# A gated attention and token-MLP block: output projection transposed, 512 tokens a matmul

## The chip, the core and the metric

The kernel runs on one core of a Trainium2 chip. The core has a matrix engine (TensorE, PE in the rows; its weight loads are PEld), VectorE (DVE), ScalarE (ACT), GpSimd (POOL), and a queue engine SyncE (SP) that only issues DMAs; 16 DMA engines move the data. The metric is the time of one execution on the device in microseconds (us).

## The reference

`x` is 2048 tokens by 640 channels. The output mixes attention and a token-mixing MLP by a gate of each token:

```python
g = _sigmoid((x * gate_w).sum(-1, keepdims=True))
a = _A_ref(x, A_wqkv, A_wo)            # 32 heads of 20 channels; softmax(q k^T * 20**-0.5) v, then @ wo
b = _B_ref(x, B_w1, B_b1, B_w2, B_b2)  # layernorm; gelu(h^T w1 + b1) w2 + b2 over the tokens
return g * a + (1 - g) * b
```

All of it is float32. The kernel keeps the precision by splitting a value into a high and a low part: a product of two split matrices takes three matmul passes (high by high, high by low, low by high).

## The kernel before

Names: P is 128, S the 2048 tokens, D the 640 channels, NC = 5 chunks of 128 channels, NT = 16 tiles of 128 tokens, HALF = 320 channels, LAST = the 4 last heads. The order of every engine's instructions is written out by hand, so each engine takes its instructions in the order of the program.

Stages, with their time in the profiled execution:

1. Up to about 222 us: the projections to q, k and v, the gate `g_t` (one value a token, tokens on the partitions), `omg` = 1 - g, and `b2o` = b2 (1 - g). Matmuls of q and k are 128x128 weights by 512 tokens (L55).
2. 222 to about 727 us: the MLP, in two halves `d` of 320 channels. In each half a phase u (w1) is followed by a phase y (w2) with 16 tiles of 128 tokens. Between its matmuls TensorE works ahead on the score maxima: matmuls `s` (L212) into four PSUM banks, which VectorE (L218, L237) or ScalarE (L227) reads. ScalarE evacuates a y tile (L708, L632), scaled by `omg` and with `b2o` added, GpSimd adds the two partial sums into `ty` (L705), and 4 us later in the planner's clock (`later_on(4000, ...)`) SyncE stores the tile to `y_d` in DRAM (L706). SyncE's queue also carries the weight loads `wr` (L518).
3. 727 to about 1699 us: the attention loop, 16 pairs of heads by 32 iterations. An iteration has four score matmuls `st`, their exponentials on ScalarE (L1022, L1030), two `s` matmuls with their maxima on VectorE until iteration 8 of the last pair, and the `pv` matmuls (L919). The row sums of the softmax go to `l_d`, the products to `o_d`; `norm_steps` makes reciprocals of the sums and stores them, broadcast to 20 rows a head, in `r_d`. In the last pair the loop also loads (`e_load`, `y_load`) and splits (`e_high`, `e_low`) what the projection needs first, and `first_row` works off the first token tile's passes with matmuls of two 64-row halves (`pair64`, L49).
4. From 1699 us: the output projection, the tail. `a_tile(t, cs)` takes 128 tokens of the normalised attention output as weights and 320 columns of `wo` as moving data, two PSUM banks a tile, four banks in turn. The attention output comes as `or` times `rb` (reciprocals), multiplied by VectorE (L966), copied to the high part by ScalarE (L968), and subtracted to the low part by VectorE (L974). The fifth chunk (k = 4) holds the last heads, whose sums are known only after the loop: `last_load`, `last_recip`, a store to `rc_d` (L881), four broadcast loads (`l_rest`, L999). Token tiles 1 to 7 therefore run four chunks first and the fifth later. VectorE evacuates with `g` times PSUM plus `oy`, the stored MLP tile (L1130), and SyncE stores 128 tokens by 640 channels of the output.

Of the kernel before, what the change touches and what calls it, by code (L numbers as in the profile page):

```python
# [13 lines left out]
P = 128  # L14
# [17 lines left out]
def gated_mix(ctx, tc, xT, x, wqk, wv0, wv1, wo, w1, w1t, b1, w2, b2, out):  # L32
# [34 lines left out]
    y_d = dram.tile([S, D], F32, name="y_d")  # L67

# [401 lines left out]
    nc.vector.tensor_mul(b2o, b2_t, omg)  # L470
    nc.scalar.activation(ssq, ssq, AF.Gelu_apprx_tanh)
# [381 lines left out]

    def norm_steps(h0, h1):
        b = (h1 - h0) * S // P
        a = S // b
        rl = ap.tile([P, 256], F32, tag="rl", bufs=1, name=f"rl{h0}")

        def load():
            nc.gpsimd.dma_start(rl[:, :b], l_d[h0:h1].rearrange("h (a b) -> (h a) b", b=b))  # L860

        def recip(i):
            nc.vector.reciprocal(rl[:, i: i + 64], rl[:, i: i + 64])
# [7 lines left out]
    last_rl = []  # L871

    def last_load():
        b = LAST * S // P
        rl = ap.tile([P, 256], F32, tag="rl", bufs=1, name="rl_last")
        nc.sync.dma_start(rl[:, :b], l_d[H - LAST:].rearrange("h (a b) -> (h a) b", b=b))
        last_rl.append(rl[:, :b])
# [12 lines left out]
    def pv_evac(p, qh, pv):  # L890
# [13 lines left out]
        if qh == 1 and p in (7, 11, 13, 15):  # L904
            h0 = {7: 0, 11: 16, 13: 24, 15: 28}[p]
# [27 lines left out]
    o_raw, o_hl, l_hl = {}, {}, {}  # L933

    def o_tiles(q, k, n, tag, bufs, names, pool, dt):
        if pool is lp:
            return [lp.tile([P, k, n], dt, tag="sq", bufs=4, name=f"{name}{tag}{q}") for name in names]
        return [pool.tile([P, k, n], dt, tag=name + tag, bufs=bufs, name=f"{name}{tag}{q}") for name in names]

    def o_load(q, rows, k, n, tag, bufs):  # L940
        raw, rb = o_tiles(q, k, n, tag, bufs, ("or", "rb"), ap, F32)
        cols = slice(q * n, (q + 1) * n)
        o_raw[q, tag] = raw, rb
        for dst, src in ((raw, o_d[rows]), (rb, r_v[rows])):
            nc.sync.dma_start(dst, src.rearrange("(c p) s -> p c s", p=P)[:, :, cols])

    tys = {}

    def y_load(t):
        if 6 <= t < 10:  # L950
            ty = q4([P, D], F32, f"oy{t}")
        else:
            n = t if t < 6 else t - 4
            if n % 3 == 0:
                shape, name = [P, 3, D], f"oy{t}"
                big_y[0] = k8(shape, F32, name) if t < 6 else lp.tile(shape, F32, tag="sk", bufs=2, name=name)
            ty = big_y[0][:, n % 3]
        tys[t] = ty
        nc.sync.dma_start(ty, y_d[t * P:(t + 1) * P, :])

    big_y = [None]

    def o_high(q, k, n, tag, bufs, pool, hi_eng):
        raw, rb = o_raw[q, tag]
        oh, ol = o_tiles(q, k, n, tag, bufs, ("oh", "ol"), pool, F32R)
        nc.vector.tensor_mul(raw, raw, rb)  # L966
        if hi_eng is nc.scalar:
            nc.scalar.activation(oh, raw, AF.Copy)  # L968
        else:
            hi_eng.tensor_copy(oh, raw)  # L970
        return oh, ol

    def o_low(q, tag, hl, eng):
        eng.tensor_sub(hl[1], o_raw.pop((q, tag))[0], hl[0].bitcast(F32))  # L974

    def e_load(q):
        o_load(q, slice(0, (NC - 1) * P), NC - 1, 256, "e", 2)

    def e_high(q, pool, eng=nc.scalar):
        o_hl[q] = o_high(q, NC - 1, 256, "e", 2, pool, eng)  # L980

    def e_low(q, eng=nc.vector):
        o_low(q, "e", o_hl[q], eng)
# [3 lines left out]
    def l_load():  # L987
# [5 lines left out]
        for q in range(4):  # L993
            o_raw[q, "l"] = raw[:, q:q + 1], rb[:, q * 512:(q + 1) * 512].unsqueeze(1)
# [38 lines left out]
    row_mms, row_ps, row_evacs = [], [], []  # L1033

    def row_half(c):
        row_ps[:] = [s_tile([P, HALF], f"a0_{c}_{k}") for k in range(2)]
        oh, ol = o_hl[0]
        cols = slice(c * HALF, (c + 1) * HALF)
        passes = [e for k in range(NC - 1) for e in ((oh[:, k, :P], woh[k]), (oh[:, k, :P], wol[k]), (ol[:, k, :P], woh[k]))]
        for i, (a, b) in enumerate(passes):  # L1040
            row_mms.append((list(row_ps), a, b[:, cols], i == 0, i == len(passes) - 1))
# [173 lines left out]
```

## Time and profile before

| | us |
|---|---|
| three runs: lowest, median, highest | 1778.77, 1779.09, 1782.85 |
| profiled execution | 1777.0 |
| its span, first to last instruction | 1775.2 |
| TensorE busy in the span | 1765.1 (99%) |
| ScalarE busy | 1483.9 (84%) |
| VectorE busy | 1225.5 (69%) |
| GpSimd busy | 658.3 (37%) |

The span is what the trace shows; 1.8 us of the profiled execution lie around it. A matmul's busy time is modelled and longer than its share of the engine: matmuls overlap, so the distance between the starts of two of them is what one costs. A row of a timeline gives the start in us from the span's begin, the time from there to the end of the last instruction that it merges, and how many (x2).

### The profile page before, as it was taken

What the parts mean: (1) busy time and instruction counts of PE and PEld (TensorE: products, weight loads), DVE (VectorE), ACT (ScalarE), POOL (GpSimd) and SP (SyncE); (2) the same over time, 40 slices, a digit from 0 to 9 for tenths busy, and PEclk for the clock granted to TensorE, in tenths of its full rate; (3) what the DMA queues carried; (4) which work ended last, traced back from release to release, by engine and by line L of the source; (5) the groups of instructions that cost most, each with busy time, mean ns of one, the idle gap of its engine ahead of it and who ended that gap; (6) DMA issues with size and microseconds to landing.
All of it is one profiled execution on the core that took longest, in us unless ns stands there. A gap on an engine that the chain in (4) does not pass through costs nothing.

```text
span 1775.2 us, 39545 instructions
## 1 busy us (share of the span) xinstructions
PE 1765.1 (99%) x15000; PEld 1091.8 (62%) x15000; DVE 1225.5 (69%) x2380; ACT 1483.9 (84%) x2566; POOL 658.3 (37%) x989
## 2 busy tenths in 40 slices
PE   9999999999999999999999999999999999999999
PEld 6998899999999999533333333333333333333378
DVE  5303289988899889777777676776767777767245
ACT  4344388888888886799999999999999999999930
POOL 1223577789877777211211111121322121212300
PEclk9999999999999999999999999999999999999999
DMA  8767876567675564334213234043353242301553
GB/s 294 251 196 244 275 179 173 144 176 206 177 195 146 159 179 145 94 67 111 65 41 85 50 72 92 12 112 68 52 136 72 50 94 59 76 15 45 198 132 135
DMA packets 155513, 225.20 MB, mean 127 GB/s; under 512 B 66420, under 2 KB 93444, under 8 KB 151640
## 3 DMA queue, kind: packets, MB, share of 16 engines
q1 hardware_dynamic: 136698, 191.70, 39.4%
q0 software_dynamic: 15888, 25.76, 6.1%
q10 hardware_dynamic: 2736, 5.21, 1.1%
q8 instruction: 118, 1.93, 0.5%
q14 instruction: 73, 0.60, 0.1%
HBM read 166.88 MB, written 55.36 MB: 125 GB/s over the span
## 4 chain that ended last, share of the span: by engine, by line
PE 95%; DMA 3%; DVE 1%; issue 0%; POOL 0%; ACT 0%; SPq 0%; DVEq 0%; ACTq 0%; POOLq 0%
PE pv L919 29%; PE st L1015 22%; PE s L212 12%; PE y L49 10%; PE u L49 9%; PE qk L55 6%; PE v L55 4%; PE a L1124 2%; DMA wr<-in_wqk_dram 1%; DMA xr<-in_xT_dram 1%; DMA rbe<-r_d 0%; DMA rc_d<-rl_last 0%; DMA k_d<-evh 0%; DVE oy L1130 0%; PE a L49 0%
## 5 line engine op out<-in xcount | busy, mean ns | idle before, releaser
L218 DVE TENSOR_REDUCE mx<-s 128x1 f32<-128x512 f32 x1280 | 834.8, 686 | 285.7 <-PE s L212 153.1
L1030 ACT ACTIVATE p<-st 128x512 f32<-128x512 f32 x1022 | 563.9, 619 | 0.0
L919 PE MATMUL pv<-p,v 128*32 128x512 f32 x4088 | 546.2, 605 | 0.0
L1022 ACT ACTIVATE p<-st 128x1024 f32<-128x1024 f32 x511 | 533.1, 1043 | 1.6 <-PE s L212 1.1
L1015 PEld LDWEIGHTS st<-qs_True,ks_True 62*128 62x128 f32 x2044 | 245.3, 185 | 433.9 <-ACT p L1022 425.9
L1015 PE MATMUL st<-qs_True,ks_True 62*128 62x512 f32 x2044 | 494.8, 446 | 0.1
L212 PE MATMUL s<-ks_False,qs_False 60*128 60x512 f32 x1152 | 362.3, 391 | 0.3 <-ACT ov L227 0.2
L44 POOL TENSOR_TENSOR wl<-wr,wh 128x512 fp32r<-128x512 f32 x228 | 275.6, 1220 | 63.9 <-ACT wh L41 52.0
L237 DVE CUSTOM_DVE_ANT_0 ov<-s,ov 128x512 f32<-128x512 f32 x384 | 263.9, 687 | 34.2 <-PE s L212 22.6
L212 PE MATMUL s<-sk,sq 60*128 60x512 f32 x896 | 281.6, 394 | 0.0
L227 ACT ACTIVATE ov<-s 128x512 f32<-128x512 f32 x384 | 228.6, 597 | 62.4 <-PE s L212 53.4
L49 PE MATMUL y<-gh,wh 64*128 64x320 f32 x896 | 225.0, 307 | 0.0
L49 PE MATMUL y<-gl,wh 64*128 64x320 f32 x832 | 216.8, 306 | 0.0
L49 PE MATMUL y<-gh,wl 64*128 64x320 f32 x832 | 216.5, 305 | 0.0
L900 POOL DMA_DIRECT2D l_d<-oev x124 | 60.8, 497 | 409.5 <-DVE oev L892 406.8
L212 PEld LDWEIGHTS s<-ks_False,qs_False 60*128 60x128 f32 x1152 | 210.4, 184 | 3.0 <-ACT ov L227 0.8
L49 PE MATMUL u<-hh,wh 64*128 64x320 f32 x864 | 206.9, 304 | 0.0
L49 PE MATMUL u<-hl,wh 64*128 64x320 f32 x864 | 206.7, 304 | 0.0
L919 PEld LDWEIGHTS pv<-p,v 128*32 128x32 f32 x4088 | 81.6, 108 | 187.3 <-issue 174.2
L49 PE MATMUL u<-hh,wl 64*128 64x320 f32 x800 | 194.4, 304 | 0.0
L41 ACT ACTIVATE wh<-wr 128x512 fp32r<-128x512 f32 (+3 forms) x247 | 146.9, 599 | 42.8 <-PE y L49 15.2
L212 PEld LDWEIGHTS s<-sk,sq 60*128 60x128 f32 x896 | 166.2, 186 | 15.3 <-DVE mx L218 0.4
(149 smaller groups left out, 2449.1 us busy)
## 6 DMA issues: line engine op xcount, KB each, us to landing
wr<-in_w_dram SPq DMA_DIRECT2D x192, 256.0 KB
ks_True<-k_d SPq DMA_DIRECT2D x96, 160.0 KB
qs_True<-q_d SPq DMA_DIRECT2D x192, 80.0 KB
qs_False<-q_d SPq DMA_DIRECT2D x96, 80.0 KB
v_d<-vt SPq DMA_DIRECT2D x32, 212.0 KB
sk<-k_d SPq DMA_DIRECT2D x42, 160.0 KB
sq<-q_d SPq DMA_DIRECT2D x84, 80.0 KB
v<-v_d SPq DMA_DIRECT2D x15, 424.0 KB
```

The source lines that it names most:

```text
L41: nc.scalar.activation(hi, src, AF.Copy)
L44: (lo_eng or nc.vector).tensor_sub(lo, src, hi.bitcast(F32))
L49: nc.tensor.matmul(ps[k], a[r], b[r], start=start, stop=stop)
L55: nc.tensor.matmul(ps, a, b, start=(i == 0 and k == 0), stop=(i == n - 1 and k == 2))
L212: nc.tensor.matmul(ps, qs[half][r, t * P:(t + 1) * P], ks[r, kc * 512:(kc + 1) * 512], start=True, stop=True)
L218: nc.vector.tensor_reduce(mx[:, slot, j, t: t + 1], ps, axis=AX.X, op=OP.max)
L227: nc.scalar.activation(over[j, kc], ps, AF.Relu)
L237: nc.vector.tensor_tensor_reduce(ov, ps, ov, 1.0, -3.0e38, OP.add, OP.max, mx[:, slot, j, t: t + 1])
L919: nc.tensor.matmul(pv[r: r + 32, :], v_tiles[p][:, kt, VW * j: VW * j + 32], pt[j, c], start=(kt == 0), stop=(kt == NT - 1))
L1015: nc.tensor.matmul(ps, ks[r, kt * P:(kt + 1) * P], qs[qh][r, c * 512:(c + 1) * 512], start=True, stop=True)
L1022: nc.scalar.activation(pt, ps, AF.Exp, scale=SCALE)
L1030: nc.scalar.activation(pt, ps, AF.Exp, scale=SCALE)
```

## The change

The projection is computed transposed: 128 channels of `wo` are the weights, 512 tokens of the attention output the moving data, and the kernel's output is [640, 2048], which the host turns back as a view. So the MLP's part must come transposed too. `y_flip` turns each `ty` in blocks of 32x32 on VectorE before the store to `y_d`; `y_turn` then turns the order of the blocks with DMAs from DRAM to DRAM on GpSimd's queue (two in each of the pairs 1 to 10). A gate value now belongs to a column, so it can't be a scalar of the evacuation: it is stored to `g_d`, loaded in the layout of the softmax sums (`load_g`) and multiplied into the reciprocals; the evacuation becomes an add. `norm` runs at pair 3 as well, with eight heads each time, since the reciprocals' tile is half as wide. The first units in the loop are two units of 512 tokens (channel tiles 0 and 1, four chunks) in place of the two halves of the first token tile. In the tail `a_bank` rotates over eight PSUM banks, `last_recip` and `l_rest` come earlier and `rc_d` is stored by SyncE's queue. The last unit runs as two of 256 tokens.

```diff
+    def y_flip(t, d, ty):
+        tt = hp.tile([P, HALF], F32, tag="tt", bufs=2, name=f"tt{d}_{t}")
+        nc.vector.transpose(tt, ty)
+        nc.sync.dma_start(y_d[t * P:(t + 1) * P, d * HALF:(d + 1) * HALF], tt)
...
-            later_on(4000, lambda: nc.sync.dma_start(y_d[t * P:(t + 1) * P, d * HALF:(d + 1) * HALF], ty))
+            later_on(4000, lambda: y_flip(t, d, ty))
...
         def recip(i):
-            nc.vector.reciprocal(rl[:, i: i + 64], rl[:, i: i + 64])
+            c = slice(i, i + 64)
+            nc.vector.reciprocal(rl[:, c], rl[:, c])
+            nc.vector.tensor_mul(rl[:, c], rl[:, c], gls[b][:, c])
...
     def last_recip():
-        nc.vector.reciprocal(last_rl[0], last_rl[0])
-        nc.gpsimd.dma_start(rc_d.rearrange("h (a b) -> (h a) b", b=LAST * S // P), last_rl[0])
+        rl = last_rl[0]
+        nc.vector.reciprocal(rl, rl)
+        nc.vector.tensor_mul(rl, rl, gls[LB][:, :LB])
+        nc.sync.dma_start(rc_d.rearrange("h (a b) -> (h a) b", b=LB), rl)
...
+    def y_turn(j):
+        nc.gpsimd.dma_start(yT_d[32 * j: 32 * j + 32].rearrange("p (u c) -> p u c", c=32),
+                            y_d[:, 32 * j: 32 * j + 32].rearrange("(u p) c -> p u c", p=32))
...
+    def l_split(*qs):
+        for q in qs:
+            o_mul(q, 2)
+            o_high(q, 2)
+        for q in qs:
+            o_low(q, 2)
+
+    def a_passes(ct, q, ks):
+        out = []
+        for k in ks:
+            oh, ol = [t[:, k % 2] for t in o_hl[q, k // 2]]
+            wh, wl = [w[k][:, ct * P:(ct + 1) * P] for w in (woh, wol)]
+            out += [(wh, oh), (wl, oh), (wh, ol)]
+        return out
...
             if p == NP - 1:
-                if it in (0, 16, 26, 30):
-                    e_load((0, 16, 26, 30).index(it))
-                if 13 <= it < 13 + NT:
-                    y_load(it - 13)
-                if it in (5, 24):
-                    e_high(it // 24, ap, nc.gpsimd)
-                    e_low(it // 24, nc.gpsimd)
+                if it in (0, 1, 13, 16, 25, 29):
+                    n = (0, 1, 13, 16, 25, 29).index(it)
+                    e_load(n // 2, n % 2)
+                if it in (2, 3, 14, 17, 19, 21):
+                    y_load((2, 3, 14, 17, 19, 21).index(it))
+                if it in (5, 7, 20, 23):
+                    e = ((0, 0), (0, 1), (1, 0), (1, 1))[(5, 7, 20, 23).index(it)]
+                    o_mul(*e)
+                    o_high(*e, nc.gpsimd)
+                    o_low(*e, nc.gpsimd)
+            elif 1 <= p < 11 and it in (8, 24):
+                y_turn(2 * (p - 1) + it // 24)
...
+    def a_unit(ct, q, ks, parts=1):
+        passes = a_passes(ct, q, ks)
+        y = yts[ct, q]
+        for i in range(parts):
+            ps = a_bank(f"a{ct}_{q}_{ks[0]}_{i}")
+            c = slice(512 * i // parts, 512 * (i + 1) // parts)
+            for n, (a, b) in enumerate(passes):
+                nc.tensor.matmul(ps[:, c], a, b[:, c], start=(n == 0), stop=(n == len(passes) - 1))
+            nc.vector.tensor_add(y[:, c], y[:, c], ps[:, c])
+            if ks[-1] == NC - 1:
+                put = (nc.scalar if i else nc.sync).dma_start
+                put(out[ct * P:(ct + 1) * P, q * 512 + c.start: q * 512 + c.stop], y[:, c])
+
+    most, full, rest = range(NC - 1), range(NC), range(NC - 1, NC)
     last_rb = l_load()
...
+    o_mul(2, 0)
+    o_mul(2, 1)
+    a_unit(2, 0, most)
+    last_recip()
+    l_rest(last_rb)
+    a_unit(3, 0, most)
+    a_unit(4, 0, most)
+    for kp in range(2):
+        o_high(2, kp)
+    for kp in range(2):
+        o_low(2, kp)
+        e_load(3, kp)
+    for ct in range(4):
+        a_unit(ct, 1, most)
+    l_split(0, 1)
+    a_unit(4, 1, most)
+    for kp in range(2):
+        o_mul(3, kp)
+        o_high(3, kp)
+    for q in (2, 3):
+        for ct in range(NC):
+            a_unit(ct, q - 2, rest)
+            if q == 2 and ct == 0:
+                l_split(2)
+            if q == 2 and ct == 2:
+                for kp in range(2):
+                    o_low(3, kp)
+            if q == 2 and ct == 4:
+                l_split(3)
+            a_unit(ct, q, full, 2 if (ct, q) == (NC - 1, 3) else 1)
```

In the new code `q` counts groups of 512 tokens, `ct` channel tiles of 128, and `kp` pairs of chunks (kp = 2 is the fifth chunk alone).

## Rows read from the trace of the kernel before

**Rows 1.** Stretches: length, busy (instructions) of five engines, clock, DMA share, GB/s.
```profile
400.00:500.00 100.00, 100.00 (x1240) 99.73 (x1240) 89.49 (x227) 84.02 (x169) 87.72 (x100) 1.00 0.71 192
...
800.00:1000.00 200.00, 200.00 (x1478) 67.92 (x1480) 140.75 (x229) 200.00 (x317) 29.07 (x64) 1.00 0.33 76
...
1699.00:1776.00 77.00, 70.36 (x456) 66.97 (x456) 43.28 (x70) 8.83 (x10) 3.69 (x7) 0.98 0.50 154
```
**Rows 2.** Timeline of PE in the tail: start, us, instruction, count, idle before.
```profile
1698.92 0.56 PE L1124 MATMUL a<-woh,ohe 128*128 128x320 f32 x2
1699.33 0.46 PE L1124 MATMUL a<-wol,ohe 128*128 128x320 f32 x2
...
1716.33 0.46 PE L1124 MATMUL a<-woh,ole 128*128 128x320 f32 x2
1717.69 0.78 PE L1124 MATMUL a<-woh,ohe 128*128 128x320 f32 x2 [0.90 <-DVE oy L1130]
...
1771.13 0.31 PE L1124 MATMUL a<-woh,oll 128*128 128x320 f32 x1
```
**Rows 3.** Timeline of PE in the q and k projections.
```profile
149.72 0.39 PE L55 MATMUL qk<-xh,wl 128*128 128x512 f32 x1
...
157.96 0.39 PE L55 MATMUL qk<-xh,wl 128*128 128x512 f32 x1
```
**Rows 4.** Timeline of DVE in the tail.
```profile
1724.01 1.22 DVE L966 TENSOR_TENSOR ore<-ore,rbe 128x1024 f32<-128x1024 f32 x1 [3.57 <-DMA rbe<-r_d]
1725.15 1.00 DVE L1130 SCALAR_TENSOR_TENSOR oy<-a,g_t,oy 128x320 f32<-128x320 f32 x2
1726.07 1.28 DVE L966 TENSOR_TENSOR orl<-orl,rbl 128x512 f32<-128x512 f32 x2
```
**Rows 5.** Groups by line and shape, whole span: busy us, mean ns, idle before.
```profile
L44 POOL TENSOR_TENSOR wl<-wr,wh 128x512 fp32r<-128x512 f32 x196 | 252.4, 1298 | 55.3 <-ACT wh L41 46.0 <-PE s L212 6.7 <-POOL xm L487 1.0
...
L180 DVE STREAM_TRANSPOSE mt<-mc 128x32 f32<-128x32 f32 x32 | 6.5, 202 | 1.2 <-POOL mc L44 1.2
...
L968 ACT ACTIVATE ohl<-orl 128x512 fp32r<-128x512 f32 x4 | 2.5, 634 | 7.3 <-DVE orl L966 7.3
```
**Rows 6.** Timelines of POOL and SP (its queue) in the tail.
```profile
1705.92 0.58 POOL L881 DMA_DIRECT2D rc_d<-rl_last x1 [0.98 <-DVE rl_last L880]
...
1713.34 1.42 SPq L999 DMA_DIRECT2D rbl<-rc_d  x4
```
**Rows 7.** Timeline of all engines at the tail's end.
```profile
1771.47 1.01 DVE L1130 SCALAR_TENSOR_TENSOR oy<-a,g_t,oy 128x320 f32<-128x320 f32 x2 [3.83 <-PE a L1124]
...
1772.52 0.35 ACTq L1133 DMA_DIRECT2D out_dram<-oy  x1
```
**Rows 8.** Timeline of ACT in the last pair: first exponential of some iterations.
```profile
1648.27 1.03 ACT L1022 ACTIVATE p<-st 128x1024 f32<-128x1024 f32 x1
...
1650.37 1.03 ACT L1022 ACTIVATE p<-st 128x1024 f32<-128x1024 f32 x1
...
1652.26 1.03 ACT L1022 ACTIVATE p<-st 128x1024 f32<-128x1024 f32 x1
...
1682.40 1.24 ACT L1022 ACTIVATE p<-st 128x1024 f32<-128x1024 f32 x1
...
1684.30 1.24 ACT L1022 ACTIVATE p<-st 128x1024 f32<-128x1024 f32 x1
```
**Rows 9.** Timelines of PE and DVE in the first y phase.
```profile
414.36 0.39 PE L212 MATMUL s<-ks_False,qs_False 60*128 60x512 f32 x1
...
416.13 0.39 PE L212 MATMUL s<-ks_False,qs_False 60*128 60x512 f32 x1
...
415.21 0.69 DVE L218 TENSOR_REDUCE mx<-s 128x1 f32<-128x512 f32 x1
```
**Rows 10.** SP's waits: who, for whom, us in all, times, longest.
```profile
SPq L706 <- POOL ty L705: 103.6, 30, 6.5
```
**Rows 11.** DMA queue of GpSimd, whole span: packets, MB, share of 16 engines.
```profile
q0 software_dynamic: 15888, 25.76, 6.1%
```

More of the change, by code (lines that the diff above doesn't have):

```diff
@@ L852, in gated_mix, with load_g @@
     s_src[NDIFF + 1] = s_stack(NDIFF + 1)
+    gls = {}
+    def load_g(b):
+        gls[b] = ap.tile([P, P], F32, tag="gl", bufs=1, name=f"gl{b}")
+        a = S // b
+        for i in range(P // a):
+            nc.gpsimd.dma_start(gls[b][a * i: a * (i + 1), :b], g_d.rearrange("t p -> (t p)").rearrange("(a b) -> a b", b=b))
     def norm_steps(h0, h1):
@@ L932, in gated_mix @@
     r_v = r_d.rearrange("h d s -> (h d) s")
[L933 to L945, printed above, removed]
@@ L973, in o_low, with e_load @@
[L973 to L983, printed above, removed]
+    o_raw, o_hl = {}, {}
+    def e_load(q, kp):
+        raw, rb = [ap.tile([P, 2, 512], F32, tag=n, bufs=2, name=f"{n}{q}_{kp}") for n in ("ore", "rbe")]
+        o_raw[q, kp] = raw, rb
+        for dst, src in ((raw, o_d), (rb, r_v)):
+            nc.sync.dma_start(dst, src[kp * 256: kp * 256 + 256].rearrange("(c p) s -> p c s", p=P)[:, :, q * 512:(q + 1) * 512])
@@ new lines, in o_mul, with o_high @@
+    def o_mul(q, kp):
+        raw, rb = o_raw[q, kp]
+        nc.vector.tensor_mul(raw, raw, rb)
+    def o_high(q, kp, eng=nc.scalar):
+        raw, _ = o_raw[q, kp]
+        if kp == 2:
+            oh, ol = [ap.tile([P, 1, 512], F32R, tag=n, bufs=4, name=f"{n}{q}") for n in ("ohl", "oll")]
+        elif q % 2:
+            oh, ol = [lp.tile([P, 2, 512], F32R, tag="sq", bufs=4, name=f"{n}{q}_{kp}") for n in ("oh", "ol")]
+        else:
+            oh, ol = [ap.tile([P, 2, 512], F32R, tag=n + "e", bufs=2, name=f"{n}{q}_{kp}") for n in ("oh", "ol")]
+        o_hl[q, kp] = oh, ol
+        if eng is nc.scalar:
+            eng.activation(oh, raw, AF.Copy)
+        else:
+            eng.tensor_copy(oh, raw)
@@ new lines, in o_low, with y_load @@
+    def o_low(q, kp, eng=nc.vector):
+        oh, ol = o_hl[q, kp]
+        eng.tensor_sub(ol, o_raw.pop((q, kp))[0], oh.bitcast(F32))
+    yts = {}
+    def y_turn(j):
+        nc.gpsimd.dma_start(yT_d[32 * j: 32 * j + 32].rearrange("p (u c) -> p u c", c=32),
+                            y_d[:, 32 * j: 32 * j + 32].rearrange("(u p) c -> p u c", p=32))
+    def y_load(n):
+        ct, i = (n, 0) if n < 4 else (4, n - 4)
+        w = S if ct < 4 else S // 2
+        if ct < 2:
+            t = k8([P, w], F32, f"yt{n}")
+        elif ct < 4:
+            t = lp.tile([P, w], F32, tag="sk", bufs=2, name=f"yt{n}")
+        else:
+            t = q4([P, w], F32, f"yt{n}")
+        nc.sync.dma_start(t, yT_d[ct * P:(ct + 1) * P, i * w:(i + 1) * w])
+        for q in range(w // 512):
+            yts[ct, i * 2 + q] = t[:, q * 512:(q + 1) * 512]
@@ L1031, in st_one, with row_unit, evac @@
         pts[g][j, 1] = pt
[L1033 to L1039, printed above, removed]
+    row_mms, row_evacs = [], []
+    def row_unit(ct):
+        ps = [s_tile([P, 512], f"a{ct}_0_{k}") for k in range(2)]
+        passes = a_passes(ct, 0, range(NC - 1))
         for i, (a, b) in enumerate(passes):
-            row_mms.append((list(row_ps), a, b[:, cols], i == 0, i == len(passes) - 1))
-        def evac(ps=list(row_ps)):
+            row_mms.append((ps, a, b, i == 0, i == len(passes) - 1))
+        def evac():
             for k in range(2):
-                nc.vector.scalar_tensor_tensor(tys[0][:, cols], ps[k], g_t[:, :1], tys[0][:, cols], op0=OP.mult, op1=OP.add)
+                nc.vector.tensor_add(yts[ct, 0], yts[ct, 0], ps[k])
         row_evacs.append(evac)
@@ L1139, in gated_mix @@
[L1139 to L1165 removed]
+    banks, two = [0], [None]
@@ new lines, in a_bank @@
+    def a_bank(name):
+        n = banks[0] % 8
+        banks[0] += 1
+        if n == 3:
+            two[0] = psum.tile([P, 2, 512], F32, tag="two", bufs=1, name=name)
+        if n in (3, 4):
+            return two[0][:, n - 3]
+        if n in (5, 6):
+            return s_tile([P, 512], name)
+        return psum.tile([P, 512], F32, tag={0: "one0", 1: "one1", 2: "s3", 7: "pv"}[n], bufs=1, name=name)
+    def a_unit(ct, q, ks, parts=1):
[10 more added lines that the diff above has]
+                put(out[ct * P:(ct + 1) * P, q * 512 + c.start: q * 512 + c.stop], y[:, c])
```

105 lines of the change are left out of this document (18 added, 87 removed).

## Prediction

> **What bounds the kernel now.** I read the windows by stage first. In the MLP TensorE is busy all of 100 us while VectorE has 10.5 us free and GpSimd 12; in the attention loop ScalarE is busy 200 of 200; in the tail, from 1699 us, only TensorE matters, ScalarE and GpSimd being almost idle [rows 1]. So the three stages have three limits: TensorE, ScalarE, TensorE. The change takes work from the tail and adds some to the other two.
>
> Next the timeline of TensorE in the tail. Its matmuls of 320 columns stand 0.1466 us apart: 58 steps of two between 1699.33 and 1716.33 [rows 2]. There are 456: tiles 1 to 7 take 12 passes each, tiles 8 to 15 take 15, the eight late chunks 3 each, 228 passes by two halves. That is 66.8 us. From the first start at 1698.92 to the end of the last slot at 1771.28 are 72.4 us [rows 2], so 5.5 us are gaps; the widest kind has PE waiting for VectorE's evacuation, since only four banks turn [rows 2].
>
> **The tail, part by part.** *Matmuls.* Eight units of 12 passes, ten of 3 and ten of 15 are 276 matmuls of 512 columns, the last 15 of them run as 30 of 256. The trace has the same form in the q and k projections, 128x128 weights by 512 columns: 36 steps from 149.72 to 157.96, 0.2289 us each [rows 3]. 261 of them are 59.7 us. For 256 columns I have only bounds: 0.119 us on the line through both widths, 0.1466 if a step never falls below that of 320. I take the line, the 30 then cost 3.6 us (up to 4.4). Together 63.3 us, 3.5 less than 66.8. Most of it is work moved into the loop: 24 passes of 512 columns there in place of 24 of 640.
>
> *Gaps.* Eight banks give VectorE seven units of time, so the waits for an evacuation should go. One new wait takes their place. The unit of channel tile 0 and tokens 1024 to 1535 is the first that needs the fifth chunk of its quarter, split by `l_split(2)`. The units before it, 84 + 12 + 3 passes, and its own first 12 are 111 steps: TensorE wants that split at 1698.92 + 25.41 = 1724.3. VectorE, in its written order after the evacuation's input of the seventh unit at 1718.2, has: that add, four operations of `l_split(0, 1)`, the next add, two `o_mul` of 1024 elements, one more add, then the multiply wanted. Operations of 512 elements come 0.6 us apart (two in 1.28), one of 1024 takes 1.14 to the next start [rows 4]; I price an add of 512 from PSUM like them. Eight of 0.6 and two of 1.14 end at 1725.3, with 0.2 us in which an add waits for its unit at 1725.5. ScalarE's copy takes 0.63 [rows 5], so TensorE starts the chunk near 1726.3, and the low part, 0.65 later, costs the third pass another 0.2. The stall is 2.2 us. Its bounds: nothing, and the present 5.5. Gaps then save 3.3 us.
>
> This holds only if the fifth chunk's loads are there. Before, the store `rc_d` went out at 1705.92 on GpSimd's queue and its readers at 1713.34 [rows 6], 7.4 us among two transfers that were issued ahead. Now it goes out on SyncE's, a microsecond sooner, ahead of the last two `e_load`s, and they can't go before VectorE's `o_low(2, ...)` near 1710. Their 2 MB at the 154 GB/s of the tail's average [rows 1] would need 14 us, to 1724, just past the 1722 and 1723 at which `o_mul(3, ...)` wants them; the tail's average includes idle time, so I count nothing, and keep 2 us for the range.
>
> *End.* Now two evacuations, 1.01 us, follow the last matmul, then the last issue at 1772.52 and the landing until 1775.2 [rows 7]. After the change one add of 256 elements follows it. From 0.6 for 512 I estimate 0.4, so 0.6 us less.
>
> **The loop.** ScalarE's first exponentials stand 1.89 us apart with a pair of `s` matmuls of 512 columns in the iteration, and 1.90 with a pair of 320 of the first units [rows 8]. The wider pairs are 24 times 0.082 = 2.0 us of TensorE; since an equal pair of `s` fits under ScalarE, nearly all hides. Three iterations carry two pairs; I take 0.5, between 0 and 2.0. An `o_mul` among the maxima cost one iteration 2.10 instead of 1.89 [rows 8]; the change has a second one there: 0.2. The two later ones come after the last maximum, and the loads for all four are issued before they are due, behind no waiting instruction of SyncE but the `m_d` ones that wait already. The multiplies by the gate are seven of 64 columns under idle VectorE: nothing.
>
> **The MLP.** 32 transposes of 128x320. The nearest row is the same operation on 32 columns, 0.202 us [rows 5]; with a column a cycle more, as in the step of 0.6 us per 512 above, 320 columns take about 0.5 us, 0.8 if twice that. One comes in every tile of 8 us, in which VectorE has 0.84 us free [rows 1]. It also has room in the banks: even a late read, 415.21 to 415.90 of the matmul at 414.36, is 0.23 us ahead of that bank's next matmul at 416.13 [rows 9], most by more. So a transpose of 0.5 can push TensorE by at most 0.3, and the free time takes most of that: I take 0.5 us in all, between 0 and 16 (nothing hidden). At the end of the MLP the last tile's transpose is ahead of the loop's first maxima on VectorE: 0.3 us (0 to 0.5). Who waits behind: `y_d`'s store on SyncE, which already waits 3.5 us a tile for GpSimd's add [rows 10], will wait some 2 to 4 us more for VectorE, and the weight loads queued behind it start later. ScalarE does not wait for those loads now; I count nothing, with up to 3 us kept.
>
> *GpSimd's DMAs.* A `y_turn` is 2048 pieces of 128 bytes. GpSimd's queue took 6.1% of 16 times 1775 us for 15888 packets [rows 11], 0.109 us a packet; at that price one turn is 14 us of the 16 engines and two fill 28 of a pair's 61 us, where a third is used [rows 1]. Nobody waits for them before the last pair. The store of the gate is as many pieces, once, in the projections. I take nothing, up to 2 us.
>
> **Sum.** -3.5 - 3.3 - 0.6 + 0.5 + 0.2 + 0.5 + 0.3 = -5.9 us: the span goes from 1775.2 to 1769.3, the profiled execution from 1777.0 to 1771.1. The median of the runs shown lies 2.1 above that execution; carried to it, 1779.1 becomes 1773.2.
>
> **Rivals.** *A wait takes the stall's place* (0.14): the last `e_load`s or `rc_d` land 2 to 4 us late, VectorE stands at `o_mul(3, ...)`, and `l_split(2)` behind it: about -3, 1776. For it speaks that such loads made VectorE wait 3.57 us before [rows 4]; against it that they now share the engines with less.
>
> *The transposes fall on TensorE* (0.06), slower. Place: both y phases. If VectorE had to wait for GpSimd's running operation, 1.30 us long [rows 5] and there 0.88 of the time [rows 1], each transpose would hold VectorE 0.5 + 0.57. What the bank's room of 0.23 and half of the 0.84 free don't take, 0.42 us, TensorE pays: 32 times that is 13 us, in place of 0.5: 1786. It decides from the point where a transpose holds VectorE for more than the 0.65 that these two take. Against it: the 32-column transposes average 0.202, half of them in the MLP beside a busy GpSimd [rows 1, 5]. The Trainium skill has this as a rule ("SBUF — State Buffer", section "SBUF: two separate sides"): VectorE in a two-port mode and GpSimd share a port pair by an exclusive lock, and the later one blocks. By that rule the time would be the 1786; the trace does not show it for the short transposes.
>
> *Late weight loads* (0.07): if the store's wait makes some splits late, +2 to +6 us against the sum, 1777 (0.05 within, 0.02 slower). *GpSimd is held* (0.03): a turn at iteration 8 stands ahead of the maxima's negation, which VectorE's transposition four iterations later waits for; if a turn keeps GpSimd more than some 18 us, every pair loses the rest, tens of us: above 1790. *More gain* (0.08): no stall at `l_split(2)`, nothing in the loop: -8 to -9, 1770.5.
>
> **Chances and range.** The forecast has 0.62, its own range -8 to -3.5, 1771 to 1775.5. A measurement can tell about 0.3%, 5.3 us, from no change. Of the forecast's chance 0.38 lie beyond that, since its centre does, and 0.24 within. Faster: 0.38 + 0.08 = 0.46. Same: 0.24 + 0.14 + 0.05 = 0.43. Slower: 0.06 + 0.02 + 0.03 = 0.11. The range from 1769 to 1780 leaves out the two slow rivals and the ends of the others.
>
> **What would show it.** In the changed profile: matmuls of the projection 0.229 us apart, TensorE's tail from start to last matmul near 65.5 us instead of 72.4, with one gap of about 2 us some 25 us into it that VectorE ends by `l_split(2)`; 32 transposes of about 0.5 us with VectorE near 95% busy in the y phases; an unchanged iteration of 1.90 us. It is wrong if gaps of more than 4 us remain in the tail, if the transposes take over 0.8 us, or if the loop begins later than 0.5 us after its present start.

## The result, and the profile after

The change made the kernel slower: 1785.83 us median (1784.11 to 1793.39, 8 runs) beside 1778.37 us for the kernel before on the same chip, a ratio of 1.0041 with a 95% interval of 1.0027 to 1.0054. In a second group it was 1.0044 (1.0029 to 1.0058). The prediction, 1773.2 us in a range of 1769 to 1780, has the wrong sign. The profiled execution took 1786.21 us, its span is 1783.8 us, 8.6 longer than before.

Where they came from is read from the starts of the same work in both traces. The operations of TensorE are the same up to the loop, so the lag of the n-th matmul can be followed:

| start of | before, us | after, us | lag | new in this stage |
|---|---|---|---|---|
| first u matmul (end of the projections) | 218.03 | 221.53 | 3.50 | **+3.50** |
| 131st u matmul | 230.87 | 237.53 | 6.66 | **+3.16** |
| first y matmul | 346.29 | 352.95 | 6.66 | 0.00 |
| 1401st y matmul (second y phase) | 612.40 | 620.34 | 7.94 | **+1.28** |
| 2561st y matmul (last tile) | 724.02 | 732.40 | 8.38 | +0.44 |
| first exponential of the loop's iterations | 727.31 | 735.68 | 8.37 | 0.00 |
| last pv matmul | 1698.40 | 1708.17 | 9.76 | +1.39 |
| last matmul of the tail | 1771.13 | 1779.88 | 8.75 | **-1.01** |
| end of the span | 1775.2 | 1783.8 | 8.55 | -0.2 |

The tail gained 1.0 us where 6.8 were forecast, and 6.66 us were lost in the first 232 us, where the forecast had counted nothing.

Stretches of the trace after (columns as in [rows 1]):

```profile
226.00:228.00 2.00, 0.11 (x3) 0.09 (x2) 0.88 (x2) 0.81 (x3) 1.26 (x1) 1.00 0.57 118
228.00:230.00 2.00, 2.00 (x18) 2.00 (x20) 1.48 (x5) 1.94 (x4) 1.05 (x1) 0.68 1.02 364
230.00:232.00 2.00, 2.00 (x17) 2.00 (x16) 1.16 (x3) 0.65 (x2) 1.48 (x2) 0.50 0.98 350
...
400.00:500.00 100.00, 100.00 (x1239) 99.72 (x1237) 92.66 (x241) 84.60 (x170) 88.27 (x100) 1.00 0.67 188
800.00:1000.00 200.00, 200.00 (x1480) 67.92 (x1472) 141.04 (x229) 200.00 (x318) 42.18 (x83) 1.00 0.40 92
1708.50:1784.00 75.50, 66.00 (x292) 52.19 (x291) 36.06 (x50) 6.74 (x8) 3.09 (x6) 1.00 0.41 129
```

VectorE's share in the y phase rose from 89.5 to 92.7% [rows 1], with TensorE at 100 as before: the transpositions are hidden there. In the tail TensorE is busy 66.0 of 75.5 us. And at 226 us TensorE stands for almost 2 us, then runs at a granted clock of 0.68 and 0.50 in the next two stretches (0.50 is the lower level, 1.2 GHz).

Timelines of POOL and SP (its queue), after:

```profile
141.56 1.19 POOL L473 DMA_DIRECT2D g_d<-g_t  x1 [6.58 <-DVE omg L471]
157.15 0.61 POOL L490 TENSOR_SCALAR xm<-xm,negm,rstd 128x320 f32<-128x320 f32 x1 [14.40 <-DMA xm<-in_x_dram]
...
145.72 0.44 SPq L330 DMA_DIRECT2D q_d<-evl  x1
146.21 0.46 SPq L485 DMA_DIRECT2D xm<-in_x_dram  x1
147.11 2.11 SPq L330 DMA_DIRECT2D q_d<-evh  x1
157.58 0.32 SPq L330 DMA_DIRECT2D q_d<-evl  x1
...
1657.03 2.38 POOL L983 TENSOR_TENSOR ol<-ore,oh 128x1024 fp32r<-128x1024 f32 x1
...
1722.34 1.67 SPq L1018 DMA_DIRECT2D rbl<-rc_d  x4
...
1725.51 0.78 SPq L961 DMA_DIRECT2D rbe<-r_d  x1
```

Timeline of DVE, after:

```profile
144.19 0.69 DVE L44 TENSOR_TENSOR evl<-qk,evh 128x512 fp32r<-128x512 f32 x1
156.86 0.69 DVE L44 TENSOR_TENSOR evl<-qk,evh 128x512 fp32r<-128x512 f32 x1 [11.99 <-DMA q_d<-evl]
...
1654.63 1.22 DVE L965 TENSOR_TENSOR ore<-ore,rbe 128x1024 f32<-128x1024 f32 x1
...
1658.42 2.07 DVE L965 TENSOR_TENSOR ore<-ore,rbe 128x1024 f32<-128x1024 f32 x1
...
1735.53 1.23 DVE L965 TENSOR_TENSOR ore<-ore,rbe 128x1024 f32<-128x1024 f32 x1 [0.49 <-DMA rbe<-r_d]
1736.67 0.68 DVE L1164 TENSOR_TENSOR yt<-yt,a 128x512 f32<-128x512 f32 x1
1737.27 0.69 DVE L965 TENSOR_TENSOR orl<-orl,rbl 128x512 f32<-128x512 f32 x1
```

The gate's store goes out at 141.56. The stores of q that SyncE issues behind it, and the loads of `xm`, do not land until about 157: VectorE stands 12 us for a buffer that a `q_d` store still reads, GpSimd gets its first `xm` at 157.15. In the kernel before the same evacuation and the same first `xm` stand at (timelines of DVE and POOL, before)

```profile
146.66 0.69 DVE L44 TENSOR_TENSOR evl<-qk,evh 128x512 fp32r<-128x512 f32 x1 [2.25 <-ACT evh L41]
146.97 0.62 POOL L487 TENSOR_SCALAR xm<-xm,negm,rstd 128x320 f32<-128x320 f32 x1 [13.23 <-DMA xm<-in_x_dram]
```

From 145 to 149 us the core's DMAs moved 3 and 19 GB/s (two stretches of 2 us), 247 and 311 in the kernel before. What the DMA list says of the store (KB, us from issue to landing):

```profile
g_d<-g_t POOLq DMA_DIRECT2D x1, 8.0 KB, 14.3
```

Timeline of PE, after, with what answers [rows 2]:

```profile
227.92 0.50 PE L214 MATMUL s<-ks_False,qs_False 60*128 60x512 f32 x1 [1.89 <-ACT ov L229]
...
1708.69 0.50 PE L1163 MATMUL a<-oh,woh 128*128 128x512 f32 x1
1709.03 0.39 PE L1163 MATMUL a<-oh,wol 128*128 128x512 f32 x1
1709.26 0.40 PE L1163 MATMUL a<-ol,woh 128*128 128x512 f32 x1
...
1735.61 0.39 PE L1163 MATMUL a<-ol,woh 128*128 128x512 f32 x1
1738.67 0.50 PE L1163 MATMUL a<-ohl,woh 128*128 128x512 f32 x1 [2.67 <-ACT ohl L977]
...
1743.64 0.40 PE L1163 MATMUL a<-oll,woh 128*128 128x512 f32 x1
1744.82 0.51 PE L1163 MATMUL a<-ohl,woh 128*128 128x512 f32 x1 [0.78 <-DVE yt L1164]
...
1779.88 0.28 PE L1163 MATMUL a<-oll,woh 128*128 128x256 f32 x1
```

Two kinds of gap are to be seen: the stall at the split of tokens 1024 to 1535 (1735.61 to 1738.67), and a wait for VectorE's add, here 1743.64 to 1744.82, which comes four times: starts 1.30, 1.18, 1.17 and, with 256 columns, 0.79 us apart.

Groups, SyncE's waits and GpSimd's queue, after, which answer [rows 5], [rows 10] and [rows 11]:

```profile
L700 DVE STREAM_TRANSPOSE tt<-ty 128x320 f32<-128x320 f32 x32 | 16.1, 504 | 0.0
```
```profile
SPq L701 <- DVE tt L700: 139.4, 31, 8.2
```
```profile
q0 software_dynamic: 17392, 31.06, 7.2%
```

The queue has 1504 packets more than in [rows 11], though twenty turns and the store, each of 2048 pieces, were added: a packet of this list is not a piece.

### The profile page after: what moved, and what is told of

The parts are those of the page before. It is cut to its first block, busy times and chain, and to the rows that moved or that the text cites. A ratio compares the mean times of both kernels' runs of the same rounds, so it can differ in the third digit from the quotient of the medians.

```text
span 1783.8 us, 39291 instructions
## 1 busy us (share of the span) xinstructions
PE 1766.7 (99%) x14835; PEld 1079.3 (61%) x14835; DVE 1231.4 (69%) x2401; ACT 1480.5 (83%) x2564; POOL 692.5 (39%) x1026
## 4 chain that ended last, share of the span: by engine, by line
PE 84%; DMA 3%; DVE 2%; POOL 0%; issue 0%; ACT 0%; SPq 0%; ACTq 0%; DVEq 0%
PE pv L941 28%; PE st L1043 22%; PE s L214 12%; PE u L49 10%; PE y L49 9%; PE a L1163 2%; DVE mx L220 1%; DMA q_d<-evl 1%; DMA k_d<-evl 1%; DMA rbe<-r_d 1%; DMA rc_d<-rl_last 0%; DMA xm<-in_x_dram 0%; PE a L49 0%; DMA k_d<-evh 0%; DVE evl L44 0%
## 5 line engine op out<-in xcount | busy, mean ns | idle before, releaser
L214 PE MATMUL s<-ks_False,qs_False 60*128 60x512 f32 x1152 | 357.1, 393 | 2.7 <-ACT ov L229 2.5
L214 PEld LDWEIGHTS s<-ks_False,qs_False 60*128 60x128 f32 x1152 | 206.6, 185 | 6.3 <-ACT ov L229 3.4
L49 PE MATMUL u<-hl,wh 64*128 64x320 f32 x864 | 199.3, 305 | 0.0
L49 PE MATMUL u<-hh,wh 64*128 64x320 f32 x864 | 199.3, 305 | 0.0
L49 PE MATMUL u<-hh,wl 64*128 64x320 f32 x800 | 186.9, 305 | 0.0
```

Source lines behind the costliest of these rows:

```text
L49: nc.tensor.matmul(ps[k], a[r], b[r], start=start, stop=stop)
L214: nc.tensor.matmul(ps, qs[half][r, t * P:(t + 1) * P], ks[r, kc * 512:(kc + 1) * 512], start=True, stop=True)
```

## Experiments

All times are beside runs of the kernel before on the same chip; a ratio is to those, with its 95% interval. Lags and the tail's difference (last pv to last matmul) are against the one trace of before, as in the table above; one trace is one execution. The executions of a kernel differ by some us, so the stages are read from the traces and the sum from the ratios.

| kernel | ratio | u first | u 131st | y 1401st | last pv | tail | span |
|---|---|---|---|---|---|---|---|
| after | 1.0041 (1.0027, 1.0054) | 3.50 | 6.66 | 7.94 | 9.76 | -1.01 | 8.55 |
| e10 after again | 1.0044 (1.0029, 1.0058) | 5.57 | 9.30 | 10.45 | 12.48 | +0.93 | 13.20 |
| e1 gate late | 1.0012 (1.0002, 1.0022) | 0.01 | -0.60 | 0.22 | 2.68 | -1.77 | 1.06 |
| e2 gate in 128 pieces | 1.0013 (1.0004, 1.0022) | -0.13 | -0.74 | 1.10 | 2.96 | -2.23 | 0.54 |
| e3 before + gate | 1.0013 (1.0005, 1.0022) | 1.95 | 4.27 | 4.25 | 4.14 | +0.96 | 5.11 |
| e6 no transposition | 1.0008 (0.9997, 1.0018) | 3.21 | 6.22 | 6.22 | 7.18 | -2.27 | 4.71 |
| e11 the same again | 1.0025 (1.0015, 1.0035) | 3.84 | 4.56 | 4.54 | 5.62 | -2.27 | 3.14 |
| e12 gate late, no transposition | 0.9993 (0.9985, 1.0002) | 1.35 | 0.95 | 1.53 | 2.62 | -0.87 | 1.54 |
| e4 banks | 1.0023 (1.0015, 1.0032) | 4.53 | 5.40 | 8.43 | 10.45 | -3.55 | 6.70 |
| e5 split first | 1.0012 (1.0002, 1.0023) | 3.05 | 7.28 | 7.35 | 9.37 | -4.79 | 4.38 |
| e7 store later | 1.0030 (1.0016, 1.0043) | 3.93 | 5.32 | 5.38 | 7.32 | -0.70 | 6.49 |
| e8 multiply later | 1.0038 (1.0026, 1.0051) | 4.79 | 5.26 | 7.73 | 8.83 | +0.20 | 8.82 |
| e9 all mends | 0.9949 (0.9937, 0.9961) | 0.67 | 0.23 | 0.27 | 1.38 | -8.72 | -7.20 |

**The gate's store, moved into the loop.**

```diff
-    nc.gpsimd.dma_start(g_d.rearrange("t p -> p t"), g_t)
...
+            if p == 0 and it == 16:
+                nc.gpsimd.dma_start(g_d.rearrange("t p -> p t"), g_t)
```

> The changed kernel with the store of the gate (g_d) issued at iteration 16 of the first pair of the attention loop instead of in the projections; nothing else differs. Theory S (the store loses the time of the start): in the trace of the changed kernel the first u matmul comes 3.5 us later than before and TensorE is 6.66 us behind by the 130th u matmul, with VectorE waiting 11.99 us for a q_d store right behind the gate's store. Then this kernel takes 6.6 us less than the changed one, about 1779, and its first u matmul stands near 218.0. Rival F (VectorE's transpositions and the stores behind them lose the time): nothing changes at the start, about 1786. Rival G (the store costs the same wherever it stands): the loop's first pair grows by what the projections gain, about 1786, with u at 218 but the second pair 6 us late.

The first u matmul is back at 218.04, the 131st is 0.60 ahead of before, and the ratio falls from 1.0041 and 1.0044 to 1.0012, 5 to 6 us. Theory S. In the loop the store still takes 11.4 us to land, and from 759 to 765 us the DMAs move 17 to 27 GB/s where the changed kernel has 143 to 149; but the loop does not lose by it: its first pair takes 61.73 us in both kernels.

**The same store at its place, in fewer pieces.**

```diff
-    nc.gpsimd.dma_start(g_d.rearrange("t p -> p t"), g_t)
+    nc.gpsimd.dma_start(g_d.rearrange("t p -> (t p)").rearrange("(p t) -> p t", t=NT), g_t)
```

> The changed kernel with the gate's store at its place, but into g_d in another order, so that it is 128 pieces of 64 bytes in place of 2048 pieces of 4 bytes; the gate's values then reach the reciprocals in a wrong order, all else is computed. Theory S, in the form that the number of pieces does it: 6 to 6.6 us less than the changed kernel, about 1779.5, and the store lands in some 2 to 4 us instead of 14.3. Rival P (the place does it: GpSimd stands 6.58 us at its wait for the gate, or the store's write itself delays the xm loads): no change, about 1786.

As good as the move: 1.0013. The DMA list and VectorE of this kernel:

```profile
g_d<-g_t POOLq DMA_DIRECT2D x1, 8.0 KB, 1.7
```
```profile
146.53 0.69 DVE L44 TENSOR_TENSOR evl<-qk,evh 128x512 fp32r<-128x512 f32 x1 [2.25 <-ACT evh L41]
```

The same 8 KB land in 1.7 us instead of 14.3, the evacuation that stood until 156.86 runs at 146.53, and from 145 to 149 us the DMAs move 295 and 293 GB/s. So it is the 2048 pieces of 4 bytes (the number is the program's; the trace does not list them one by one), not the place or GpSimd's wait.

**The store alone, in the kernel before.**

```diff
     nc.vector.tensor_mul(b2o, b2_t, omg)
+    nc.gpsimd.dma_start(g_d.rearrange("t p -> p t"), g_t)
```

> The kernel before with the gate's store added at the place that it has in the changed kernel, and nothing else of the change; nobody reads what it stores. Theory S: 5.5 to 6.7 us slower than before, about 1784.5, with the first u matmul 3.5 us later and the first y matmul 6.6 us later. Rival F or another part of the change as the cause: within 1 us of before, 1778 to 1779.

Its trace lags 4.27 us by the 131st u matmul and no further; but the median is only 2.2 us over before (interval 0.9 to 3.9), and the traced execution was the slowest of its eleven. The sign is settled, the size is not: in the eight traces of changed kernels with this store the same lag is 4.6 to 9.3. The hold itself is as long here, VectorE's evacuation waits 11.3 us for the `q_d` store (11.0 to 13.1 in those eight). Why the median loses less by it than the 5 to 6 us of e1 and e2 stays open.

**The transpositions left out.**

```diff
-        nc.vector.transpose(tt, ty)
-        nc.sync.dma_start(y_d[t * P:(t + 1) * P, d * HALF:(d + 1) * HALF], tt)
+        nc.sync.dma_start(y_d[t * P:(t + 1) * P, d * HALF:(d + 1) * HALF], ty)
```

> The changed kernel without VectorE's 32 transpositions: the MLP's tiles are stored as they are, so the MLP's part reaches the output in a wrong order; all else is computed. Theory S: TensorE's lag in the two y phases did not grow in the changed kernel (6.66 us at the first y matmul and at the last of half 0), so the transpositions themselves cost nothing there; what they cost is the wait of the store for VectorE, behind which SyncE's weight loads start 2 to 5 us later and TensorE loses 1.2 us at the start of the second half's u phase, and 0.4 and 0.4 us around the MLP's end: 1.5 to 2 us less than the changed kernel, about 1784. Rival F (the transpositions are the main loss): 6 us less or more, 1780 or under.

> Once more the kernel without VectorE's transpositions (the MLP's part reaches the output in a wrong order), now beside the changed kernel itself. By the stages of its first trace it should be 1.5 to 3 us under the changed kernel; its first median was 5.9 us under that of an earlier group. If it is again 5 us or more under, the transpositions cost more than the stages show, through the start or the tail; if 1.5 to 3, the first median had caught executions in which the gate's store cost less.

> The changed kernel with the gate's store in the first pair and without VectorE's transpositions (the MLP's part reaches the output in a wrong order): the price of the transpositions where the store does not disturb. By the stages: 0.4 at the MLP's last tile, 0.4 in the first iterations of the loop, 0.7 at the start of the second half's u phase: 1.5 us under the kernel with the late store alone, about 1778, as the kernel before. If the transpositions cost more than that (5 us), 1774.

The first group gave 1.0008, more than expected; beside the changed kernel itself it was 3.4 us under it (1.0044 to 1.0025), and without the store's disturbance 3.4 us again (e1 to e12: 1.0012 to 0.9993), each to within some 3 us. The stages give about 2.2 us of it: the lag grows between the 131st u and the 1401st y matmul by 0.0 in e6 and e11 and by 0.6 in e12, but by 1.3, 1.2, 0.8, 1.8, 3.0, 0.1 and 2.5 in the seven kernels with transpositions whose stores follow at once (mean 1.5). The last tile is another 0.42 to 0.44 us later in every kernel with a transposition, and the first two iterations of the loop together 0.44 longer.

**The stores of the transposed tiles later.**

```diff
         nc.vector.transpose(tt, ty)
-        nc.sync.dma_start(y_d[t * P:(t + 1) * P, d * HALF:(d + 1) * HALF], tt)
+        def put():
+            nc.sync.dma_start(y_d[t * P:(t + 1) * P, d * HALF:(d + 1) * HALF], tt)
...
+            later_on(4000, put)
```

> The changed kernel with the store of each transposed tile issued 4 us later in the planner's clock than its transposition, instead of right behind it. Theory Q (SyncE's queue stands at the store until VectorE has transposed, and the weight loads behind it come late at the start of the second half's u phase): the loads are issued 2 to 5 us earlier in the y phases, the 1.2 us at 510 to 518 us are regained, about 1784.6. Rival (the loads are late for another reason, or the loss there is VectorE's): no change, 1785.8.

Set against TensorE's own lag, the 58 weight loads of the first y phase are issued 2.96 us later in the changed kernel (1.45 to 5.34), within 0.1 us of their old place without transpositions, and about 0.9 earlier here (the mean of each). SyncE's waits in this kernel and in e6:

```profile
SPq L703 <- DVE tt L700: 65.7, 24, 8.8
```
```profile
SPq L699 <- POOL ty L711: 102.9, 30, 6.5
```

So the wait of [rows 10], grown from 103.6 to 139.4 us, is what delays the loads. Here the lag does not grow at 510 us (5.32 to 5.38), but e5 lost only 0.1 there with loads as late as in the changed kernel: whether late loads cost TensorE 0 or 3 us is a matter of the execution, and one trace does not show that the later store saves the loss.

**The banks in another order.**

```diff
-        n = banks[0] % 8
+        n = (0, 1, 2, 3, 5, 6, 4, 7)[banks[0] % 8]
```

> The changed kernel with another order of the eight banks in the tail: the two banks that are halves of one tile no longer follow each other. Theory B: four times in the tail TensorE's next unit stands until VectorE's add of the unit before is done (1719.56, 1743.64, 1761.23 and 1777.33 us in the changed kernel's trace), always at the change from the first to the second half of that tile, so the wait is for the tile, not for the data. In all 3.9 us; without them 2.5 to 3.9 us less, 1782 to 1783.3, since what is saved ahead of the fifth chunk's split may come back as a wait for it. Rival (VectorE itself is late with its adds, as in the kernel before): the waits move to other units, within 0.7 us of the changed kernel.

```profile
1719.56 0.39 PE L1163 MATMUL a<-ol,woh 128*128 128x512 f32 x1
1719.79 0.39 PE L1163 MATMUL a<-oh,woh 128*128 128x512 f32 x1
```

In this timeline of PE the first unit that waited runs on, and all four waits are gone; of PE's gaps in the tail over half a microsecond only the one at the split is left, 3.26 us from start to start and 0.59 for the next step. The tail is 2.5 us shorter than in the changed kernel, although its steps stand 0.43 us apart for some 3 us behind that stall (below). Each of the two is one trace; the absence of the gaps is the proof, not the 2.5.

**The split first.**

```diff
     a_unit(4, 1, most)
+    l_split(2)
     for kp in range(2):
         o_mul(3, kp)
...
-            if q == 2 and ct == 0:
-                l_split(2)
```

> The changed kernel with the split of the fifth chunk for tokens 1024 to 1535 written ahead of the two multiplies of 1024 elements for tokens 1536 to 2047. Theory V (VectorE's written order makes the stall at 1735.61 us): the multiplies with their wait of 0.49 us no longer stand ahead of it, the stall of 3.06 us goes, 2.8 to 3.2 us less, about 1782.8. Rival R1 (the loads of the fifth chunk are what is late): the stall stays over 1.5 us, with VectorE waiting for a DMA of rbl, and at most 1.5 us are gained, 1784.5 or more.

```profile
1731.25 0.39 PE L1163 MATMUL a<-ol,woh 128*128 128x512 f32 x1
1731.48 0.40 PE L1163 MATMUL a<-ohl,woh 128*128 128x512 f32 x1
1731.72 0.40 PE L1163 MATMUL a<-ohl,wol 128*128 128x512 f32 x1
```

In this timeline of PE the chunk that waited runs on without a gap. The tail is 3.8 us shorter than in the changed kernel (the ratios give 5 for the whole, more than the 2.8 to 3.2 expected, with other losses at 510 us), so VectorE's order made the stall, not the loads: in the changed kernel these land up to 9.9 us after their issue, but in time for the new order.

**The second multiply one iteration later.**

```diff
-                if it in (5, 7, 20, 23):
+                if it in (5, 8, 20, 23):
```

> The changed kernel with the second multiply of the loop's last pair (1024 elements) at iteration 8 instead of 7. In the changed kernel's trace that multiply took 2.07 us, the one at iteration 5 took 1.2, and it overlaps GpSimd's subtraction from 1657.03 to 1659.41 us: 2.07 is 0.99 of waiting until that subtraction's end and 1.08 of work. Theory L (VectorE's multiply is held by GpSimd's running subtraction): at iteration 8 it starts behind the subtraction and takes about 1.2 us, the iteration of 2.74 us falls to about 2.1, 0.6 us less in all. Rival (VectorE has no room for a second multiply among the maxima, or an operation of 1024 elements takes 2.07 us here anyway): some iteration of the pair stays at 2.5 us or more. 0.6 us is little for the median; the periods of the iterations in the trace decide.

```profile
1660.43 1.22 DVE L965 TENSOR_TENSOR ore<-ore,rbe 128x1024 f32<-128x1024 f32 x1
```

On VectorE's timeline the multiply takes 1.22 us again, and the iterations 8 and 9, from one's first exponential to the next one's, take 1.89 and 1.87 us where the changed kernel has 2.74 and 1.87: 0.85 gained, even more than expected, since a multiply written at iteration 8 costs nothing at all. The hold does not rest on one event. In all ten traces of changed kernels that keep the multiply at iteration 7 it takes 2.06 to 2.08 us and ends 1.08 to 1.09 behind GpSimd's subtraction. At iteration 23 a multiply and a subtraction start within 0.02 us of each other, and one of them always waits for the whole of the other: in the changed kernel the subtraction takes 3.48 us beside a multiply of 1.22, in e1, e7, e9 and e12 the multiply takes 3.47 to 3.48 beside a subtraction of 2.40.

**All mends, and one unit moved ahead of the late loads.**

```diff
+    a_unit(0, 2, most)
     for q in (2, 3):
         for ct in range(NC):
             a_unit(ct, q - 2, rest)
...
-            a_unit(ct, q, full, 2 if (ct, q) == (NC - 1, 3) else 1)
+            a_unit(ct, q, rest if (ct, q) == (0, 2) else full, 2 if (ct, q) == (NC - 1, 3) else 1)
```

> The changed kernel with five mends together: the gate's store in the first pair of the loop, the banks in the other order, the split for tokens 1024 to 1535 ahead of the multiplies, each transposed tile's store 4 us after its transposition, the second multiply at iteration 8; and one unit (channel tile 0, tokens 1024 to 1535) runs its first four chunks ahead of everything that needs the fifth, so that TensorE has 2.7 us of work more before it needs the late loads. If the stages add up: the start 0.5 us ahead of the kernel before, the last tile of the MLP and the first iterations of the loop 0.8 late, the last pair 0.7 late, the tail 6.5 to 7.5 shorter than before: about 6 us under the kernel before, 1772. Rival (the loads of the fifth chunk take the place of the stall): TensorE waits 1 to 3 us for the split of tokens 0 to 511, 1774 to 1775.

1769.4 us (1768.5 to 1769.82) beside 1778.75: 0.9949, 9 us under the kernel before and faster than both kernels; 6 were expected, and the one trace has 7.2. The rival did not come: the tail's matmuls, first start to last, take 63.48 us with 0.2 us of gaps.

> The changed kernel itself once more, beside the others of this group, for what differs from execution to execution: 5 to 8 us above the kernel before. What is read from its trace: the start's loss (5.3 to 7.3 us in the six traces with the gate's store in small pieces, 4.3 in the kernel before with the store alone), the tail (1.8 us shorter to 0.2 longer than before in the five traces with the same tail), and whether TensorE's steps stand at 0.43 us instead of 0.229 after the stall near 28 us into the tail.

The start's loss is 9.30 us in this trace and its tail 0.93 longer than before, both beyond what the earlier traces had shown. The tail of the same code varies by 3.2 us over nine traces, -2.27 to +0.93, and these stretches of e10's trace show the largest part of it:

```profile
1738.50:1741.70 3.20, 0.44 (x2) 0.00 (x1) 2.42 (x3) 2.37 (x3) 0.00 (x0) 1.00 0.12 45
1742.50:1743.50 1.00, 1.00 (x4) 0.84 (x5) 0.48 (x1) 0.00 (x0) 0.00 (x0) 0.98 0.00 0
1743.60:1746.90 3.30, 3.30 (x9) 2.59 (x8) 0.79 (x2) 0.00 (x0) 0.00 (x0) 0.50 0.43 159
1747.00:1750.00 3.00, 2.22 (x10) 1.53 (x9) 0.69 (x1) 0.00 (x0) 0.00 (x0) 1.00 0.00 0
```

Behind the stall TensorE gets a clock of 0.50 for 3.3 us, nine matmuls 0.43 us apart. The rest is the stall, 2.33 to 3.21 us from start to start.

## Why the prediction was wrong, step by step

Two of the prediction's own three signs of being wrong came: gaps of over 4 us remained in the tail, and the loop began 8.4 us later.

- **The gate's store, "as many pieces, once, in the projections. I take nothing, up to 2 us".** This is the step that failed most: 6.66 us in the trace, 5 to 6 by the ratios of e1 and e2, 2.2 when the store alone is added to the kernel before. What was wrong is its cover. The windows that are shown [rows 1] begin at 400 us, and of the projections only TensorE's steps [rows 3]; their stores of q and loads of `xm` stood behind the store, and their evacuations wait for those stores. A price of the right size was there, 14 us of all 16 engines for 2048 pieces beside the 14.3 that the store took, but by luck: it was worked out per packet, a packet of that queue is not a piece, and the turns, priced at the same 14, landed in 4.0 to 8.6. The 3.16 us after the first u matmul are the same loss arriving later, for e1 and e2 have none of it: ScalarE's evacuations wait for `k_d` transfers and weight loads, TensorE stands 1.89 us and then gets half the clock. The Trainium skill, "DMA: Bandwidth & Descriptors", section "Why small descriptors are slow (HBM only)", names fixed overheads of each packet and each descriptor, of which concatenating spares a part; e2 agrees with it in kind, 14.3 against 1.7 us, but the section has no price for 4 bytes, and the prediction did not use it.
- **Gaps of the tail, 5.5 to 2.2.** They came to 7.9 us (the distances of starts over 0.229, or over 0.119 for 256 columns, summed). "Eight banks give VectorE seven units of time, so the waits should go" is the failed step: `a_bank` makes two of the eight banks halves of one tile, and a matmul into its second half waited until the add from the first was done, four times, 3.6 us, and another 0.4 in the slow first steps behind them. The code shows it; the prediction counted banks and not tiles. e4 shows it: without that order the gaps are gone.
- **The stall at `l_split(2)`, 2.2 us.** Right in place and cause, a little small: 2.8 us and 0.4 in the steps behind it, with 0.5 more at the first unit of the fifth chunk. The waits of VectorE for `rbl` (0.55) and `rbe` (0.49) added to the order, a mild form of the first rival; `rc_d` took 7.0 us to land from SyncE's queue, where its readers had waited 7.4 behind GpSimd's [rows 6], so the move to the other queue hardly shortened it. The prediction let the last `e_load`s go out as soon as `o_low(2, ...)` allowed, near 1710 on the old clock and 1720 here; they went out at 1724.06 to 1725.51, since in SyncE's queue they stand behind `l_rest`, which waited for `rc_d` until 1722.34. e5 gives the whole stall to VectorE's order.
- **Matmuls, -3.5.** Right: 0.229 us a step, 0.12 for 256 columns as on the line that was taken, and 63.5 us in e9 against 63.3. ("24 of 640" in the prediction is a slip: in the loop before there are 24 passes of 320 columns, as its 2.0 us for the wider pairs reckon.) Of the 3.5, by an estimate, 2.1 are the 4608 columns that moved into the loop, at the tail's 0.1466 us per 320 [rows 2], and only 1.4 the cheaper column of a wider matmul.
- **End, -0.6.** Measured -0.2. The add of 256 took 0.42 as estimated, but from the last matmul's start to the span's end are 3.9 us against 4.1 [rows 2, 7], since the transfer behind the add landed later.
- **The loop.** The wide pairs, 0.5: iterations 14, 18 and 26 of the last pair, which carry two pairs, took 2.08, 2.12, 2.12 against 1.91, 1.95, 1.95, which is 0.5: right. The second `o_mul`, 0.2: it cost 0.84, since it met GpSimd's subtraction (e8). With the 0.44 of the first two iterations, which is the transpositions', that makes 1.8; the loop lost 1.39, since four later iterations of the last pair are 0.04 shorter each and its last matmul follows 0.2 sooner on the last exponential. The other pairs: 1.897 to 1.898 us an iteration before and after, so the turns cost nothing, and they landed in 4.0 to 8.6 us, not 14.
- **The transpositions, 0.5 us in all.** One takes 0.504 us, as estimated, and in the y phases the lag does not grow (6.66 at the first y matmul and at the 1281st). But 0.44 us at the last tile and the late loads, a rival of 0.07 with 2 to 6 us, came on top: the loads' 1.3 us here, 0 to 3 over the traces. "ScalarE does not wait for those loads now; I count nothing" was the step. The seam, the first two iterations of the loop, was 0.44, forecast 0.3.
- **The rival by GpSimd's lock.** Right that it would not fall on the transpositions: 499 to 513 ns, though 27 of the 32 started with up to 1.14 us of a GpSimd operation still to run. But the prediction looked for the lock at the wrong instruction. The multiply of two tiles in SBUF started at 1658.42, GpSimd's subtraction ended at 1659.41, and 2.07 us is 0.99 of waiting and 1.08 of work. The Trainium skill, "SBUF — State Buffer", section "SBUF: two separate sides", names just this pair: a VectorE operation with two inputs in SBUF against a GpSimd operation that reads SBUF, and the later one waits for the whole instruction. It agrees with both rows, and read closely it would have priced the multiply; the transposition has one input, and its rows show no hold. The prediction's "by that rule the time would be the 1786" took for granted that a transposition is one of the cases that the rule names.

Summed with what was measured, 6.66 + 1.28 + 0.44 + 1.39 - 1.01 - 0.2 = 8.6 us of span. e9 takes the losses back and keeps the gain, a tail 8.7 us shorter, less 0.5 for the wider pairs in the loop. But little of that is 512 columns a matmul: 1.4 us are, 2.1 are work moved into the loop, and the other 5.2 are gaps that went with eight banks in a good order, an earlier split and a unit moved ahead. Whether the kernel before could lose its gaps in the same way was not tried, so what the transposed form itself is worth stays open.

## What to carry to other kernels

Price every transfer that a change adds in pieces, not bytes, and look at the stretch in which it is issued, above all at one that the change does not seem to be about: 8 KB held up the core's transfers for 14 us. Where buffers are counted against waits, count what the program waits for, the tile, and not the hardware's units. An operation added between others is priced by what runs beside it on the engine that shares its path, and a store that has to wait is priced by the queue behind it.

## What the hardware showed that was not expected

- 2048 pieces of 4 bytes from SBUF to DRAM took 13.3 to 15.1 us in nine traces, and an evacuation that waited for a transfer issued behind them stood 11.0 to 13.1 us; the same 8 KB in 128 pieces took 1.7.
- A VectorE multiply of 128x1024 with both inputs in SBUF was held for the rest of a running GpSimd subtraction (2.07 us instead of 1.22), and a subtraction for the whole of a multiply (3.48 instead of 2.38); transpositions with one input never were (0.50 us, 27 of 32 begun beside a running GpSimd operation).
- After a stall of 2.3 to 3.3 us in the tail TensorE's steps stood 0.43 us apart for 2 to 4 us in five of ten traces (e4, e7, e8, e10, e12; the granted clock of e10 is shown above), and in the other five (after, e1, e2, e6, e11) they did not, though the tail's program is the same in nine of them. It adds up to 2 us to one execution of the same kernel.
